# DeltaNet and a GELU layer on one core: chunk 5's squares at another place, chunk 1's tokens added on VectorE, chunk 1's joins two units at a time

## The chip, the core and the metric

The kernel runs on one core of a Trainium2 chip. The core has TensorE (matrix products, PE in the profile, its weight loads PEld), VectorE (DVE), ScalarE (ACT), GpSimd (POOL) and SyncE (SP, which issues most DMAs). Products are written to PSUM, and VectorE and ScalarE read them from there. The metric is the time of one execution on the device in microseconds.

## What is computed

A DeltaNet attention (4 batches, 8 heads, 768 steps, head size 48) is followed by two dense layers with an exact GELU between them:

```python
for t in range(S):
    kt, vt, bt = (k_n[:, :, t], v[:, :, t], beta[:, :, t, None])   # k_n = k / (|k| + 1e-6)
    y[:, :, t] = np.einsum('bhd,bhde->bhe', q[:, :, t], state)
    v_old = np.einsum('bhde,bhd->bhe', state, kt)
    state = state + bt[:, :, :, None] * np.einsum('bhd,bhe->bhde', kt, vt - v_old)
...
h = x @ w_in                       # x: y as 3072 tokens of 384; w_in 384 x 2048
g = 0.5 * h * (1.0 + erf(h * inv_sqrt2))
return (g @ w_out)                 # w_out 2048 x 384
```

Both weight matrices come as 64-bit floats and are decoded on the chip.

## The kernel before

The 768 steps are cut into 12 chunks of 64. A chunk has two units (`NA` = 2; unit `a` holds batches 2a and 2a+1 on the two halves of the partitions, with 8 heads). Two chunks form a pair `g`. For a pair, the products of keys with keys ("grams", `psG`) give triangular systems. Their 32x32 diagonal blocks are inverted on VectorE, row by row (`eliminate`, L489 to L503, then transposes L512 and L516). The off-diagonal 32x32 block is filled by two small levels of products, the "joins" (`psJ`): level 0 multiplies gram and inverse and is scaled by VectorE into `XM`; level 1 multiplies that with the inverse and is copied by ScalarE into `Zf`.

A chunk then goes through `against_state` (products of keys and queries with the state, `psK`; L661 to L668), `subtract` (L672: `W` = those of the keys minus V, on VectorE; `y` = those of the queries, copied by ScalarE), `solve` (`psU`), `use` (`psY`, and the state's update into the same tile), `next_state` (L748, VectorE) and `read` (L750: the tokens `x` out of `psY`). `turn` (L766) transposes x into `xT`, and the two dense layers follow. Chunk 0 has no state to read, so its `y` is empty. For chunk 1, x and y are kept apart and added on TensorE, by two products with the identity into one PSUM tile (L776). For later chunks, `read` adds y on VectorE and `turn` transposes once (L779).

The first joins of chunk 1 use `join` (L538): one product per unit, half and level, into a tile of the two-bank tag `dn`. The later pairs use `join_run` (L575): two neighbouring units in one product with 64 columns, of which the two diagonal blocks are read out, each by an instruction of its own; its level 1 copies are recorded with `put_off` and issued later by `copy_out`.

The norm of a chunk's keys, from chunk 4 on, takes three steps: `norms(c)` (L333: two ScalarE squares, one per unit, into `ksq` tiles that share the tag `x` with the tokens), `prep(c)` (L345: two row sums on VectorE, L349, and a power with exponent 0.5 on GpSimd, L351), and `finish(c)` for the pair (L303 to L307 on VectorE: reciprocals and the factors `gm`).

The two dense layers of chunks 0 and 1 are plain products (`fc1` L811, `fc2` L829). From chunk 2 on they are products of blocks with sums and differences of blocks (names P1 to R22 in `part_of_layer`, L906, products at L916; second layer at L859). The sums of the weights are VectorE's (L842, L846, L874). Product P4 writes on into the PSUM tile Y1, which VectorE's L947 must have read before; L939 and L968 read it earlier.

The order of the work is written by hand up to L1173. From L1196 on it is a plan: each step has a time on a scale in which chunk c's dense layers run from c+1 to c+2 (chunk 0's to 2.25), and all steps are issued in the order of these times. VectorE keeps that order as written; the other engines are ordered by a scheduler that follows it but may move an instruction that it takes to be ready ahead of one that isn't. ScalarE instructions issued through `keep` or `copy_out` stay in their order among themselves, and the products of `together` follow one another. Every engine runs its instructions in the final order. Weights of the first layer are decoded up to L1172 and from plan time 0.99 to 1.36, those of the second from 1.365 to 1.9 (VectorE L231 to L261, ScalarE L237).

Of the kernel before, what the change touches and what calls it, by code (L numbers as in the profile page):

```python
# [19 lines left out]
def kernel(  # L20
# [28 lines left out]
    nc = tc.nc  # L49
# [517 lines left out]
    def put_off(name, dst, src):  # L567
        copies[name].append((dst, src))
# [6 lines left out]
    def join_run(g, ts0, ts1):  # L575

        xm, zf, off = XMs[g], Zf[g % 2], Gs[g]
        gm = gms[g].rearrange("q t h -> q (t h)")
        sets = []
        both = dn("psJ") if g > 1 and ts0 else None  # L580
        for level, ts in enumerate((ts0, ts1)):
            if ts:
                if both is not None:
                    psJ = both[:, level]
                else:
                    psJ = small[0].tile([128, 512], F32, tag="sq" if level else "z", name="psJ")
                sets.append((level, ts[0] * H, psJ.rearrange("q (k n) -> q k n", n=2 * HB)))
        for k in range(H):
            for p in range(2):
                for level, u0, psJ in reversed(sets):  # L590
                    us = slice(u0 + 2 * k, u0 + 2 * k + 2)
                    rows = slice(p * C + level * HB, p * C + (level + 1) * HB)
                    nc.tensor.matmul(psJ[HALF[p], k, :],  # L593
                                     lhsT=(xm if level else off)[rows, us, :],
                                     rhs=zf[rows, us, HB:C] if level else xm[rows, us, :],
                                     start=True, stop=True)
        for level, u0, psJ in sets:
            for p in range(2):
                for e in range(2):
                    us = slice(u0 + e, u0 + 2 * H, 2)  # L600
                    at_ = p * C + e * HB
                    src = psJ[at_:at_ + HB, :, e * HB:(e + 1) * HB]
                    if level == 0:
                        low_ = slice(p * C + HB, (p + 1) * C)
                        nc.vector.tensor_tensor(
                            xm[low_, us, :], src,
                            gm[low_, us].unsqueeze(2).to_broadcast([HB, H, HB]), op=ALU.mult)
                    else:
                        put_off("join", zf[p * C:p * C + HB, us, HB:C], src)

    def gram_steps(c, part=(0,)):
        us = [tiles[c, a] for a in range(NA)]
# [38 lines left out]
    def against_state(us):  # L651

        for u in us:
            u.W = wk.tile([128, H, D], F32, tag="W", name="W")
            u.y = None
            if u.c == 0:
                nc.gpsimd.tensor_tensor(u.W, u.V,
                                        ng[:, u.a].unsqueeze(2).to_broadcast([128, H, D]),
                                        op=ALU.mult)
                continue  # L660
            u.psK = dn("psK")[:, :, 0:2 * NP * D].rearrange("q r (x j d) -> q x r j d", x=2, d=D)  # L661
            for x in range(2):
                for j in range(NP):
                    for r, p in QUADS:
                        rows = slice(r * C, r * C + D)
                        to = HALF[p ^ (j % 2)] if x and u.c > 1 else HALF[p]
                        nc.tensor.matmul(u.psK[to, x, r, j, :], lhsT=(u.Qt if x else u.Kt)[rows, p, j, :],  # L667
                                         rhs=St[rows, u.a, p ^ r, j, :], start=True, stop=True)  # L668
        if us[0].c > 2:
            subtract(us)  # L670
# [79 lines left out]
    def read(u, copy=nc.scalar.copy):  # L750
        u.x = wk.tile([128, H, D], F32, tag="x", name="x")
        both = slice(0, 128)
        for to, at_, s in ((both, both, 0), (HALF[0], HALF[1], 1), (HALF[1], HALF[0], 1)):
            dst, src = pairs(u.x[to], s), u.psY[s][at_]
            if u.c < 2:
                copy(dst, src)
            else:
                nc.vector.tensor_tensor(dst, src, pairs(u.y[at_], s), op=ALU.add)
# [7 lines left out]
    def turn(u):  # L766
        if u.a == 0:
            xTs[u.c] = wk.tile([128, NM, NA * 128], F32, tag="xT", name="xT")
        xT = xTs[u.c]
        psX = sq("psX", NM, 128)  # L770
        for m in range(NM):
            cols = slice(m * 128, (m + 1) * 128)
            if u.c == 1:

                for i, part in enumerate((u.x, u.y)):
                    nc.tensor.matmul(psX[:, m, :], lhsT=part.rearrange("q h d -> q (h d)")[:, cols],  # L776
                                     rhs=ident, start=i == 0, stop=i == 1)
            else:
                nc.tensor.transpose(psX[:, m, :], u.x.rearrange("q h d -> q (h d)")[:, cols], ident)  # L779
        nc.scalar.copy(xT[:, :, u.a * 128:(u.a + 1) * 128], psX)  # L780

    def turns(us):
# [271 lines left out]
    def at(first, last, steps):  # L1054

        total, done, timed = sum(s[0] for s in steps), 0.0, []
        for w, *step in steps:
            timed.append((first + (last - first) * (done + 0.5 * w) / total, step))
            done += w
        return timed  # L1060
# [128 lines left out]
    def state_at(c, *times, first=(), second=()):  # L1189

        steps = state_steps(c, first, second)
        if len(times) > len(steps):
# [4 lines left out]
    plan += [decode_in(), at(1.365, 1.9, decode_steps(n_in, NW)), at(1.91, 1.911, [(1.0, late)])]  # L1197
    rows1, join1 = eliminate_steps(1), join_steps(1)
    plan += [at(1.06, 1.065, [(1.0, load, 3)]),
             [(t, (join, 0, range(NA, 2 * NA), level)) for level, t in enumerate((1.085, 1.16))],  # L1200
]
    sums = [(1.0, sum_of_squares, tiles[3, a], h) for a in range(NA) for h in range(H)]
    plan += [at(1.48, 1.8, sums), at(1.81, 1.811, [(1.0, fn, c) for c in (2, 3) for fn in (norms, prep)]), at(1.9, 1.905, [(1.0, finish_both)]), at(2.725, 2.726, [(1.0, queries, third)]),
# [61 lines left out]
    for w in range(3, NC):  # L1265
        two_ahead = w + 2 < NC
        if w % 2:
            if w == 3:
                plan += [at(w + 0.19, w + 0.191, [(1.0, transposed, u, (1,)) for u in fourth]),
                         at(w + 0.1, w + 0.101, [(1.0, together, *gram(5))]),  # L1270
                         at(w + 0.06, w + 0.061, [(1.0, norms, 5), (1.0, prep, 5)]),
                         at(w + 0.11, w + 0.111, [(1.0, finish, 4)])]
                plan += rows_of(2, w, ((1, 0.112, 0.113), (2, 0.16, 0.2), (4, 0.224, 0.31),
                                       (2, 0.325, 0.365), (1, 0.395, 0.4), (2, 0.485, 0.5),
                                       (2, 0.508, 0.54), (5, 0.6, 0.685), (7, 0.76, 0.88),
                                       (3, 1.0, 1.05), (5, 1.07, 1.1), (1, 1.153, 1.154),
                                       (1, 1.2, 1.201), (1, 1.201, 1.202)))
            elif two_ahead:
                plan += rows_of(w // 2 + 1, w, ((1, -0.35, -0.349), (1, -0.34, -0.339),
                                                (1, -0.23, -0.229), (5, -0.22, -0.14),  # L1280
                                                (1, -0.07, -0.06), (3, 0.005, 0.05),
                                                (3, 0.068, 0.148), (2, 0.156, 0.215),
                                                (2, 0.235, 0.31), (3, 0.325, 0.365),
                                                (1, 0.398, 0.409), (2, 0.485, 0.5),
                                                (1, 0.508, 0.54), (5, 0.6, 0.685),
                                                (3, 0.76, 0.8), (1, 1.003, 1.004),
                                                (1, 1.16, 1.161), (1, 1.166, 1.167)))
            plan += [state_at(w, w + 0.367, w + 0.59, w + 0.72, w + 0.93, second=query(w))]
        else:
            j0, j1, j2 = join_steps(w // 2)  # L1290
            t = w + (0.25 if w == 4 else 0.165)
            plan += [at(t, t + 0.001, [(1.0, together, j0, *query(w))]),
                     at(w + 0.37, w + 0.371, [(1.0, together, j1, *gram(w + 2))]),
                     state_at(w, w + 0.465, w + 0.58, w + 0.72, w + 0.93, second=[j2] + gram(w + 3))]
            plan += spread("join", 4, w + 0.395)
            plan += spread("join", 4, w + 0.64)
            if two_ahead:
                plan += spread("gram", 2, w + 0.375) + spread("gram", 2, w + 0.42)
                plan += spread("gram", 4, w + 0.63)
                plan += [at(w + 0.366, w + 0.367, [(1.0, norms, w + 2)]), at(w + 0.3715, w + 0.372, [(1.0, prep, w + 2)]),  # L1300
                         at(w + 0.56, w + 0.561, [(1.0, norms, w + 3), (1.0, prep, w + 3)]),
                         at(w + 0.64, w + 0.641, [(1.0, finish, w + 2)])]
# [32 lines left out]
```

## Time and profile before

| | |
|---|---|
| time, median of 3 runs | 646.0 us (645.03 to 646.12) |
| the profiled execution | 644.96 us, of which the span is 643.2 us |
| TensorE busy (matmul) | 617.9 us, 96% of the span, 9702 records |
| VectorE busy | 496.3 us, 77%, 1011 instructions |
| ScalarE busy | 259.9 us, 40%, 586 instructions |
| GpSimd busy | 66.0 us, 10%, 58 instructions |
| mean granted TensorE clock | 0.985 |

The page gives the busy share in 40 equal slices of 16.1 us, in tenths:

```profile
PE   6759999999989999999999999999999999999997
DVE  6999989989589997999577999577999565354342
ACT  4576767524632256132266132266132253132230
POOL 4044002001301003001003001013001000000000
PEclk9987999999989999999999999999999999999999
```

The first 160 us hold the hand-written start, the decoding of the weights and chunks 0 and 1; then chunks 2 to 11 follow with TensorE nearly always busy. A matmul of 32-bit floats shows as two records in the trace, a transpose as one.

### The profile page before, as it was taken

What the parts mean: (1) busy time and instruction counts of PE and PEld (TensorE: products, weight loads), DVE (VectorE), ACT (ScalarE), POOL (GpSimd) and SP (SyncE); (2) the same over time, 40 slices, a digit from 0 to 9 for tenths busy, and PEclk for the clock granted to TensorE, in tenths of its full rate; (3) what the DMA queues carried; (4) which work ended last, traced back from release to release, by engine and by line L of the source; (5) the groups of instructions that cost most, each with busy time, mean ns of one, the idle gap of its engine ahead of it and who ended that gap; (6) DMA issues with size and microseconds to landing.
All of it is one profiled execution on the core that took longest, in us unless ns stands there. A gap on an engine that the chain in (4) does not pass through costs nothing.

```text
span 643.2 us, 22156 instructions
## 1 busy us (share of the span) xinstructions
PE 617.9 (96%) x9702; PEld 573.8 (89%) x9702; DVE 496.3 (77%) x1011; ACT 259.9 (40%) x586; POOL 66.0 (10%) x58
## 2 busy tenths in 40 slices
PE   6759999999989999999999999999999999999997
PEld 5658876776879999999999999999999999999997
DVE  6999989989589997999577999577999565354342
ACT  4576767524632256132266132266132253132230
POOL 4044002001301003001003001013001000000000
PEclk9987999999989999999999999999999999999999
DMA  9794683204422335312325312411211400100100
GB/s 135 174 273 159 129 199 113 45 1 74 84 37 42 56 43 91 58 24 37 66 34 86 61 21 41 67 21 33 51 25 35 69 3 3 25 2 3 25 2 24
DMA packets 158433, 39.79 MB, mean 62 GB/s; under 512 B 150016, under 2 KB 153216, under 8 KB 158336
## 3 DMA queue, kind: packets, MB, share of 16 engines
q1 hardware_dynamic: 155664, 37.34, 30.0%
q10 hardware_dynamic: 2672, 1.03, 0.8%
q8 instruction: 76, 1.25, 0.8%
q14 instruction: 21, 0.17, 0.1%
HBM read 33.62 MB, written 4.72 MB: 60 GB/s over the span
## 4 chain that ended last, share of the span: by engine, by line
PE 77%; DVE 14%; DMA 2%; issue 2%; SPq 2%; ACT 1%; POOL 1%; DVEq 0%; POOLq 0%
PE psX L859 12%; PE psY L916 11%; PE psY L859 8%; PE psX L916 8%; PE psV L916 5%; PE psZ L916 5%; PE psZ L859 4%; PE psV L859 4%; PE psK L667 3%; DVE Nu L503 3%; DVE tmp L501 3%; PE psG L414 3%; PE psJ L593 3%; PE psH L811 2%; PE psY L732 2%
## 5 line engine op out<-in xcount | busy, mean ns | idle before, releaser
L916 PE MATMUL psX<-xT,w_in_sb 128*128 128x128 f32 x480 | 64.8, 278 | 0.0
L503 DVE TENSOR_TENSOR Nu<-Nu,tmp 128x58 f32<-128x58 f32 (+13 forms) x168 | 57.9, 344 | 5.8
L501 DVE TENSOR_TENSOR tmp<-Nu 128x58 f32<-128x58 f32 (+13 forms) x168 | 58.0, 345 | 4.4
L916 PEld LDWEIGHTS psX<-xT,w_in_sb 128*128 128x128 f32 x480 | 59.4, 193 | 0.9
L902 ACT COPY xT<-psX 128x768 f32<-128x768 f32 x9 | 7.2, 799 | 124.3 <-PE psX L788 124.3
L351 POOL TENSOR_TENSOR n<-n,half 128x16 f32<-128x16 f32 x10 | 31.4, 3145 | 251.8 <-DVE n L349 191.2
L859 PE MATMUL psX<-w_out_sb,G 128*128 128x192 f32 x320 | 55.3, 326 | 0.0
L859 PEld LDWEIGHTS psX<-w_out_sb,G 128*128 128x128 f32 x320 | 52.1, 190 | 0.0
L811 PE MATMUL psH<-xT,w_in_sb 128*128 128x256 f32 x192 | 45.2, 390 | 0.5 <-ACT G L902 0.4
L829 PE MATMUL psO<-w_out_sb,G 128*128 128x384 f32 x128 | 43.9, 490 | 0.0
L811 PEld LDWEIGHTS psH<-xT,w_in_sb 128*128 128x128 f32 x192 | 36.3, 193 | 8.0 <-ACT G L902 1.3
L916 PE MATMUL psY<-xT,w_in_sb 128*128 128x128 f32 x320 | 43.1, 279 | 0.0
L916 PEld LDWEIGHTS psY<-xT,w_in_sb 128*128 128x128 f32 x320 | 39.8, 196 | 0.0
L902 ACT COPY pu<-psZ 128x512 f32<-128x512 f32 x40 | 23.5, 587 | 39.3 <-PE psZ L916 37.7
L829 PEld LDWEIGHTS psO<-w_out_sb,G 128*128 128x128 f32 x128 | 23.6, 190 | 14.0
L902 ACT ACTIVATE G<-G 128x512 f32<-128x512 f32 x40 | 25.2, 630 | 23.3 <-DVE G L947 22.6
L939 DVE TENSOR_TENSOR psY<-psY,pu 128x512 f32<-128x512 f32 x20 | 14.0, 698 | 22.4 <-PE psY L916 19.6
L376 POOL TENSOR_TENSOR V<-V,n 128x384 f32<-128x384 f32 x18 | 17.0, 959 | 135.4 <-DMA V<-in_v_dram 115.5
L859 PE MATMUL psZ<-T,pu 128*128 128x192 f32 x160 | 28.6, 332 | 0.0
L859 PE MATMUL psY<-T,G 128*128 128x192 f32 x160 | 28.6, 332 | 0.0
L859 PE MATMUL psV<-w_out_sb,G 128*128 128x192 f32 x160 | 27.7, 326 | 0.0
L859 PE MATMUL psX<-T,G 128*128 128x192 f32 x160 | 27.6, 326 | 0.0
(183 smaller groups left out, 1346.1 us busy)
## 6 DMA issues: line engine op xcount, KB each, us to landing
Kp<-in_k_dram SPq DMA_DIRECT2D x76, 96.0 KB, 3.2
w_out_sb<-in_moe_w_in_dram SPq DMA_DIRECT2D x24, 256.0 KB, 4.1
w_raw<-in_moe_w_out_dram SPq DMA_DIRECT2D x16, 384.0 KB, 4.5
V<-in_v_dram SPq DMA_DIRECT2D x48, 96.0 KB, 3.1
out_dram<-o_sb SPq DMA_DIRECT2D x40, 96.0 KB, 2.2
Qp<-in_q_dram SPq DMA_DIRECT2D x64, 32.0 KB, 2.1
Qp<-in_q_dram SPq DMA_DIRECT2D x16, 96.0 KB, 4.7
Qp<-in_k_dram SPq DMA_DIRECT2D x32, 32.0 KB, 2.2
```

The lines of the kernel that those rows point to most:

```text
L351: nc.gpsimd.tensor_tensor(flat, flat, half, op=ALU.pow)
L376: engine.tensor_tensor(u.V, u.V, ns[u.c][:, u.a].unsqueeze(2).to_broadcast([128, H, D]), op=ALU.mult)
L414: nc.tensor.matmul(psG[HALF[p], r, i * NP + j, :], lhsT=u.Kt[rows, p, j, :], rhs=(u.Qt if x else u.Kt)[rows, p, j, :], start=True, stop=True)
L501: nc.vector.tensor_tensor(tmp, nu[:, j + 1:, j:j + 1].to_broadcast([128, n, j]), nu[:, j:j + 1, 0:j].to_broadcast([128, n, j]), op=ALU.mult)
L503: nc.vector.tensor_tensor(nu[:, j + 1:, 0:j], nu[:, j + 1:, 0:j], tmp, op=ALU.add)
L593: nc.tensor.matmul(psJ[HALF[p], k, :], lhsT=(xm if level else off)[rows, us, :], rhs=zf[rows, us, HB:C] if level else xm[rows, us, :], sta ...
L667: nc.tensor.matmul(u.psK[to, x, r, j, :], lhsT=(u.Qt if x else u.Kt)[rows, p, j, :], rhs=St[rows, u.a, p ^ r, j, :], start=True, stop=True)
L811: nc.tensor.matmul(psH, lhsT=w_in_sb[:, f // 2, m, f % 2 * 128:(f % 2 + 1) * 128], rhs=xTs[c][:, m, :], start=(m == 0), stop=(m == NM - 1))
L829: nc.tensor.matmul(u.psO, lhsT=G[:, u.a, f, :], rhs=w_out_sb[:, f, :], start=(f == 0), stop=(f == NF - 1))
L859: nc.tensor.matmul(ps_, lhsT=lhs[:, f, :], rhs=rhs[:, f, :], start=first and f == 0, stop=f == FH - 1, skip_group_check=not first)
L902: i = fn(*args, **kw)
L916: nc.tensor.matmul(ps_[:, i], lhsT=lhs[:, f // 2, f % 2 * 128:(f % 2 + 1) * 128], rhs=rhs, start=first and i == 0, stop=True, skip_group_c ...
```

## The change

The squares and row sums of chunk 5 are put at other plan times: `norms(5)` from 3.06 to 2.93, right behind chunk 2's turn (2.922), and `prep(5)` from 3.06 to 2.961, right behind `last_sum_of_w` (L846, 2.96). `finish(4)` stays at 3.11, `sum_of_w(4)` (L842) at 3.07.

Chunk 1's tokens are read like those of later chunks: `read` adds y on VectorE (six additions in place of six ScalarE copies), `turn` transposes x alone, and `against_state` puts the query products of chunk 1 on the partitions that this addition needs.

Chunk 1's two joins (plan times 1.085 and 1.16, unchanged) use `join_run`, with PSUM tiles of the one-bank tag `sq`, and their level 1 copies are issued at once.

```diff
@@ join_run
-                    psJ = small[0].tile([128, 512], F32, tag="sq" if level else "z", name="psJ")
+                    psJ = small[0].tile([128, 512], F32, tag="sq" if level or g == 0 else "z",
+                                        name="psJ")
...
-                        put_off("join", zf[p * C:p * C + HB, us, HB:C], src)
+                        put = put_off if g else lambda name, to, at: nc.scalar.copy(to, at)
+                        put("join", zf[p * C:p * C + HB, us, HB:C], src)
@@ against_state
-                        to = HALF[p ^ (j % 2)] if x and u.c > 1 else HALF[p]
+                        to = HALF[p ^ (j % 2)] if x and u.c > 0 else HALF[p]
@@ read
-            if u.c < 2:
+            if u.c < 1:
                 copy(dst, src)
             else:
                 nc.vector.tensor_tensor(dst, src, pairs(u.y[at_], s), op=ALU.add)
@@ turn
-            if u.c == 1:
-
-                for i, part in enumerate((u.x, u.y)):
-                    nc.tensor.matmul(psX[:, m, :], lhsT=part.rearrange("q h d -> q (h d)")[:, cols],
-                                     rhs=ident, start=i == 0, stop=i == 1)
-            else:
-                nc.tensor.transpose(psX[:, m, :], u.x.rearrange("q h d -> q (h d)")[:, cols], ident)
+            nc.tensor.transpose(psX[:, m, :], u.x.rearrange("q h d -> q (h d)")[:, cols], ident)
@@ the plan
-             [(t, (join, 0, range(NA, 2 * NA), level)) for level, t in enumerate((1.085, 1.16))],
+             [(1.085, (join_run, 0, range(NA, 2 * NA), ())),
+              (1.16, (join_run, 0, (), range(NA, 2 * NA)))],
...
-                         at(w + 0.06, w + 0.061, [(1.0, norms, 5), (1.0, prep, 5)]),
+                         at(w - 0.07, w - 0.069, [(1.0, norms, 5)]), at(w - 0.039, w - 0.038, [(1.0, prep, 5)]),
```

In the last lines w is 3.

## The prediction

> **What bounds the kernel now.** I read the busy times by stretch first, then TensorE's waits, then each engine's timeline around the three places of the change. The stretches (columns: stretch, length, busy time and instruction count of TensorE matmul, TensorE load, VectorE, ScalarE, GpSimd, granted TensorE clock, DMA share, GB/s):
>
> ```profile
> 71.50:88.00 16.50, 16.47 (x369) 14.11 (x370) 14.70 (x23) 13.03 (x28) 0.00 (x0) 1.00 0.62 116
> 93.00:110.00 17.00, 17.00 (x62) 11.32 (x62) 16.70 (x24) 11.41 (x36) 2.94 (x1) 1.00 0.52 160
> 176.00:180.00 4.00, 0.01 (x1) 0.00 (x0) 3.83 (x8) 0.01 (x1) 1.61 (x2) 1.00 0.38 46
> 180.00:184.50 4.50, 4.49 (x25) 4.49 (x26) 4.36 (x7) 1.69 (x3) 0.00 (x0) 0.62 0.35 42
> 184.50:260.00 75.50, 75.50 (x1453) 73.17 (x1453) 66.11 (x139) 31.36 (x64) 9.79 (x6) 1.00 0.35 54
> ```
>
> TensorE is full nearly everywhere. It stands still once, from 176 to 180, and pays again afterwards: its clock is granted at 0.62 in the next 4.5 us. From 93 to 138 VectorE is as full as TensorE. The hole at 176, on GpSimd, VectorE and TensorE (start, us, engine, line, operation, wait before it):
>
> ```profile
> 168.60 0.70 DVE L939 TENSOR_TENSOR psY<-psY,pu 128x512 f32<-128x512 f32 x1 [2.77 <-ACT diag L425]
> 169.40 0.69 DVE L968 TENSOR_TENSOR pu<-psY,pu 128x512 f32<-128x512 f32 x1
> 170.40 1.01 DVE L349 TENSOR_REDUCE n<-ksq 128x8 f32<-128x384 f32 x2 [0.30 <-ACT ksq L902]
> 171.33 1.75 DVE L842 TENSOR_TENSOR T<-w_out_sb,T 128x1536 f32<-128x1536 f32 x1
> 175.87 0.18 DVE L303 TENSOR_SCALAR n<-n 128x32 f32<-128x32 f32 x1 [2.79 <-POOL n L351]
> 179.27 0.68 DVE L947 TENSOR_TENSOR G<-psY,pu 128x512 f32<-128x512 f32 x1
> ...
> 171.49 4.35 POOL L351 TENSOR_TENSOR n<-n,half 128x16 f32<-128x16 f32 x1 [10.76 <-DMA Kp<-in_k_dram]
> ...
> 180.01 1.56 PE L916 MATMUL psY<-TX,w_in_sb 128*128 128x128 f32 x8 [4.00 <-DVE G L947]
> ```
>
> This is chunk 5's norm: squares on ScalarE at 169.84, row sums on VectorE (L349), the square root as a power on GpSimd (L351), then VectorE's factors (L303). L947, which frees the PSUM tile that product P4 needs, is queued behind the factors on VectorE, so TensorE waits 4.00 us. The power's releaser is named as a DMA, but the row sums end at 171.41, 0.08 us before it: they are the real releaser. VectorE also idled 2.77 us at 168.60.
>
> Chunk 1's tokens (ScalarE reads them out, TensorE turns x and y) and the next join:
>
> ```profile
> 86.79 0.56 DVE L748 TENSOR_TENSOR St<-St,psY 128x384 f32<-128x384 f32 x1 [1.21 <-PE psY L743]
> 87.72 0.56 DVE L748 TENSOR_TENSOR St<-St,psY 128x384 f32<-128x384 f32 x1 [0.38 <-PE psY L743]
> 88.20 0.95 DVE L260 SCALAR_TENSOR_TENSOR w_e<-w_raw,w_e 128x768 uint32<-128x768 uint32 x1
> ...
> 137.95 1.15 PE L593 MATMUL psJ<-XM,G 32*64 32x64 f32 x32 [0.48 <-DVE XM L512]
> ```
>
> From 88.20 VectorE decodes weights and then eliminates, without a gap over 0.25 us, until TensorE waits 0.48 us for it at 137.95.
>
> [...] Here the three transposes of chunk 2's unit take 0.33 us (160.98 to the next product at 161.31), the twelve matmul records of chunk 1's unit 1.34 us (88.98 to 90.32). [...] the power took 4.35 us beside L842, which reads two SBUF tensors, and 2.90 us at 157.82, with nothing of the kind beside most of it.
>
> **Part A, the squares sooner.** It moves two ScalarE squares (0.94 us) from behind chunk 4's grams to behind chunk 2's turn, the two row sums (1.01 us) and the power from behind L968 to behind L846; no DMA is issued with them. Chunk 5's keys are there: their four loads are issued from 149.59 to 153.52 and land 2.8 to 4.0 us later. The squares' buffers are chunk 2's x tiles, free after the transposes (last start 162.04). So the squares run from about 163.1, in a ScalarE gap of 1.46 us before 164.56. Row sums: L846 ends at 165.83, so 165.85 to 166.87, inside VectorE's 2.77 us idle time before 168.60; hidden, and if that cover were gone it would cost 1.0. Power: 166.9 to 169.8 at 2.90 (171.3 at 4.35). L842 then follows L968 at 170.1 and ends at 171.85; both powers are done by then, so the factors start at 171.87 instead of 175.87: 4.0 us. From there to L947's end is 179.95-175.87 = 4.08 us, so P4 may start at 176.0. TensorE's previous product (174.95, 1.06 long) ends at 176.0 too. The 4.0 us wait goes. The cold tail goes too: from 180.01 to 184.42 three groups of eight took 4.41 us, where a warm group goes every 0.89 (185.31 to 186.21): 4.41-2.67 = 1.7 us. What is late next: VectorE gains only 4.0 where TensorE gains 5.7, and at 228.77 the next join needs VectorE's transpose, which ends at 228.36. VectorE has 0.93 (L939 at 186.48) and 0.38 (190.25) of idle time to catch up; 0.4 slack and 1.3 idle cover 1.7. I charge 0.2. The earlier squares also release the key buffers for SP's next loads (171.00) earlier, which nothing waits for. Part A: -5.5, between -5.7 and -4.0 (tail kept).
>
> **Part B, tokens and Y added on VectorE.** Off ScalarE: six copies, 1.96 us, beside its other work, worth nothing. On VectorE: six adds, for which chunk 2's L758 is the row: 1.08 and 1.09, together 2.17. They stand in the queue between the two state additions and ahead of L260; 0.38 of it falls into the wait before 87.72. So VectorE's decode is late by 1.8. Off TensorE: 2 x (1.34-0.33) = 2.0. New waits: x waits for VectorE instead of ScalarE (second unit ready at 90.0, formerly 89.3), and w_out's second decoded block, used at 90.32, is ready at 91.9 instead of 90.1. TensorE may stand there up to 2.6 us unless other products are ordered ahead of it. That TensorE runs full from 93 to 137.5 makes its saved 2.0 worth something only if the join at 137.95 isn't governed by VectorE. It is: VectorE comes at 137.8+1.8 = 139.6. Behind the join VectorE had one wait on TensorE, 1.15 us at 145.06, which can take up part. Cost: from +0.4 (that wait absorbs 1.15 and part of the filler is ordered ahead) to +1.9, and below nothing (-0.5) only if the products' order lets the saved 2.0 through. I take +1.1. The other PSUM half for Y (L666) costs nothing: same products.
>
> **Part C, joins with two units to a product.** TensorE: 64 records in 1.13 us (60.83 to 61.96) become 32 in about 1.07 (137.95 to 139.02), twice: -0.1. VectorE: two multiplications of 0.70 become four of 0.42-0.43: +0.33, in front of the second join, for which TensorE waits already (0.48 at 66.12). ScalarE: two copies of 0.58 become four of 0.36: +0.3, mostly in the 0.33 idle before 68.85. VectorE's extra is swallowed by its 1.21 us wait at 86.79. The psJ tile moves to a tag idle from 55 to 88. Cost 0 to +0.4; I take +0.2.
>
> **Sum.** -5.5+1.1+0.2 = -4.2 on the profiled execution (644.96 us, span 643.2), so 640.8. The shown median is 646.0, 1.0 above it; I forecast against the median: 641.8.
>
> **Rivals.** (1) Part A yields less because the chain is only moved: the power slow, or L842 and the factors still later than P4, a second hole of some 2 us. For it: VectorE is 99% full around there. Against it: 2.77 us idle ahead of it. A is then about -3.3, net -2.0: 644.0. (2) Both parts gain: TensorE's saved 2.0 is used, because the products are ordered anew around the join, so B is -0.5 and A -5.7; net -6.2, 639.8. Against it: VectorE is just as full. (3) Slower: the start-up becomes VectorE's, with new holes in TensorE at 66, 89 and 136, each followed by a cold tail of 1.7 as at 180. Price: 1.8+0.3+3 x 1.7 = 7.2, against -5.5: +1.7, 647.7. It decides once each hole passes the idle time that the clock tolerates (between 1 us, which left it at 1.00 at 66, and 4.0). Against it: holes at 89 and 136 are 2.6 and some 4 us at most if nothing fills them, and products of the dense layers are there to fill them.
>
> **How the numbers follow.** Forecast 0.66, rival 1 0.16, rival 2 0.08, rival 3 0.10. About 0.2% (1.3 us) is what this kernel's measurement tells from no change. Of rival 1, 0.06 lies within it, of rival 3 0.02: faster 0.84, same 0.08, slower 0.08. The forecast's own ends are 646.0-5.3 = 640.7 and 646.0-1.7 = 644.3; the range reaches a little to rival 2: 640.0 to 644.6.
>
> **What would show it.** Right: chunk 5's squares near 163, power before 170, P4 with no wait over 0.3 us and a granted clock near 1.00 after 176; six L758 adds at 87 to 90 on VectorE; the join of 137.95 some 0.5 to 2 us later. Wrong: a wait on L947 or L303 that stays, a new TensorE hole over 3 us at 89 or 136 with a lowered clock behind it, or the join at 228 waiting over 0.5 us for VectorE.

## The result, and the profile after

The changed kernel takes 645.68 us in the median, the kernel before 645.7 us, each in 19 runs taken side by side. The ratio is 0.9991 with a 95% interval of 0.9982 to 0.9999: a gain of some 0.6 us, of 1.2 us at most by the interval, where 4.2 us were forecast. The profiled execution has the same span as before, 643.2 us. The runs of the changed kernel spread over 3.35 us (643.58 to 646.93), those of the kernel before over 1.64 us.

The hole at 176 is gone. The busy times of the changed kernel by stretch (columns as in the prediction: TensorE matmul and load, VectorE, ScalarE, GpSimd, granted clock, DMA share, GB/s):

```profile
138.00:164.40 26.40, 24.40 (x547) 17.59 (x548) 21.71 (x29) 9.06 (x21) 1.29 (x1) 0.87 0.23 43
...
176.00:180.00 4.00, 4.00 (x38) 4.00 (x37) 3.83 (x7) 3.21 (x6) 1.61 (x2) 1.00 0.58 108
180.00:184.50 4.50, 4.50 (x42) 4.50 (x41) 4.46 (x5) 2.56 (x5) 0.00 (x0) 1.00 0.31 39
```

From 176 to 184.5 TensorE is full and its clock is whole, where it stood and then ran at 0.62. But the stretch from 138 to 164.4 now has 2.0 us of idle TensorE and a clock of 0.87. The timeline of the changed kernel shows both places (start, us, engine, line, operation, and the wait before it):

```profile
89.22 1.09 DVE L760 TENSOR_TENSOR x<-psY,y 128x192 f32<-128x192 f32 x3
90.34 0.96 DVE L260 SCALAR_TENSOR_TENSOR w_e<-w_raw,w_e 128x768 uint32<-128x768 uint32 x1
137.88 1.97 DVE L512 STREAM_TRANSPOSE XM<-Nu 128x1024 f32<-128x1024 f32 x1
140.00 1.15 PE L594 MATMUL psJ<-XM,G 32*64 32x64 f32 x32 [2.95 <-DVE XM L512]
141.08 0.72 PE L669 MATMUL psK<-St,Kt 48*64 48x48 f32 x32
142.43 1.08 PE L669 MATMUL psK<-St,Kt 48*64 48x48 f32 x32
144.29 4.88 PE L825 MATMUL psO<-w_out_sb,G 128*128 128x384 f32 x8
...
168.28 0.94 ACT L898 ACTIVATE ksq<-Kp 128x384 f32<-128x384 f32 x2
169.64 1.05 PE L912 MATMUL psX<-xT,w_in_sb 128*128 128x128 f32 x8
171.03 1.01 DVE L349 TENSOR_REDUCE n<-ksq 128x8 f32<-128x384 f32 x2
172.11 2.90 POOL L351 TENSOR_TENSOR n<-n,half 128x16 f32<-128x16 f32 x1 [6.10 <-DVE n L349]
176.95 0.17 DVE L303 TENSOR_SCALAR n<-n 128x32 f32<-128x32 f32 x1
181.13 1.12 PE L912 MATMUL psY<-TX,w_in_sb 128*128 128x128 f32 x8
183.87 1.06 PE L912 MATMUL psZ<-TX,Sw 128*128 128x128 f32 x8
```

The same places in the kernel before:

```profile
135.71 2.09 DVE L512 STREAM_TRANSPOSE XM<-Nu 128x1024 f32<-128x1024 f32 x1
139.52 0.65 PE L667 MATMUL psK<-St,Qt 48*64 48x48 f32 x32
141.03 2.85 PE L829 MATMUL psO<-w_out_sb,G 128*128 128x384 f32 x8
164.36 1.05 PE L916 MATMUL psX<-xT,w_in_sb 128*128 128x128 f32 x8
184.42 1.06 PE L916 MATMUL psZ<-TX,Sw 128*128 128x128 f32 x8
```

Read the lower half of the changed kernel's lines first. The squares start right behind chunk 2's turn, the power takes 2.90 us and ends at 175.01, the factors (L303) follow L838 with no wait, and P4 follows the product ahead of it with no wait. From the first product P1 of chunk 2 to P5 of the second block it is 14.23 us (169.64 to 183.87), before 20.06 (164.36 to 184.42): the squares gain 5.83 us.

Now the upper half. VectorE takes up its decode at 90.34 instead of 88.20. It reaches the transpose L512 at 137.88 instead of 135.71. The join that waits for it starts at 140.00 instead of 137.95, and TensorE stands for 2.95 us instead of 0.48. Behind the join TensorE is slow: each 32 records of psK take 0.85 us from start to start (142.43 to 143.28) instead of about 0.47, and the eight records of psO 4.88 us instead of 2.85.

P1 of chunk 2 starts 5.28 us later than before. That splits as follows. The join is 2.05 us late; 0.37 of that is there already at VectorE's first addition to chunk 1's state (87.16 instead of 86.79), ahead of the tokens, and 1.7 come behind it. From the join's start to the start of the next join it takes 9.09 us (140.00 to 149.09) instead of 5.86 (137.95 to 143.81), 3.23 us more. From there to P1 it is 20.55 us in both. So 5.28 us are lost before P1 and 5.83 gained behind it. The 0.55 us that remain at P5 are lost again by the end (459.3 us from P5 to the end of the span, before 458.8).

### The profile page after: what moved, and what is told of

It reads as the page before. It is cut to its first block, busy times and chain, and to the rows that moved or that the text cites. A ratio compares the mean times of both kernels' runs of the same rounds, so it can differ in the third digit from the quotient of the medians.

```text
span 643.2 us, 21991 instructions
## 1 busy us (share of the span) xinstructions
PE 620.4 (96%) x9620; PEld 573.9 (89%) x9620; DVE 498.3 (77%) x1019; ACT 257.8 (40%) x582; POOL 64.7 (10%) x58
## 4 chain that ended last, share of the span: by engine, by line
PE 78%; DVE 16%; issue 2%; ACT 1%; DMA 1%; POOL 0%; SPq 0%; DVEq 0%; ACTq 0%; POOLq 0%
PE psX L855 12%; PE psY L912 11%; PE psX L912 8%; PE psY L855 8%; PE psV L912 5%; PE psZ L912 5%; PE psZ L855 4%; DVE tmp L501 4%; DVE Nu L503 4%; PE psV L855 4%; PE psK L669 4%; PE psO L825 3%; PE psG L414 3%; PE psJ L594 3%; PE psU L704 2%
## 5 line engine op out<-in xcount | busy, mean ns | idle before, releaser
L825 PE MATMUL psO<-w_out_sb,G 128*128 128x384 f32 x128 | 46.5, 510 | 0.3 <-DVE w_out_sb L261 0.2
L807 PE MATMUL psH<-xT,w_in_sb 128*128 128x256 f32 x192 | 46.5, 395 | 0.2
```

Of the source, the lines that this page charges most:

```text
L807: nc.tensor.matmul(psH, lhsT=w_in_sb[:, f // 2, m, f % 2 * 128:(f % 2 + 1) * 128], rhs=xTs[c][:, m, :], start=(m == 0), stop=(m == NM - 1))
L825: nc.tensor.matmul(u.psO, lhsT=G[:, u.a, f, :], rhs=w_out_sb[:, f, :], start=(f == 0), stop=(f == NF - 1))
```

## The experiments

Theory 1: the squares gain in full. The tokens on VectorE make the join near 138 late, TensorE stands ahead of it for so long (2.95 us) that its clock falls behind the hole, and the slow products there cost more than the lateness itself. Theory 2: there is no such step. Either only VectorE's lateness counts, or the hole at 176 was never worth its 5.8 us.

All kernels were profiled and timed beside the kernel before. Profiled executions of one source differ by up to 1.5 us already at the end of the hand-written start (the join of the squares alone starts at 138.13 in one and 139.65 in the other), so the table gives lengths within one execution. "Wait" is TensorE's idle time right ahead of the join near 138. "Join to P1" is the time from that join's start to P1 of chunk 2. "P1 to P5" reaches to P5 of the second block.

| kernel | ratio to before (95%) | wait | join to P1 | P1 to P5 |
|---|---|---|---|---|
| before | 1 | 0.48 | 26.41 | 20.06 |
| changed | 0.9991 (0.9982 to 0.9999) | 2.95 | 29.64 | 14.23 |
| squares alone | 0.9902 (0.9889 to 0.9915) | 0.49 | 26.42 | 14.22 |
| tokens alone | 1.0060 (1.0048 to 1.0072) | 2.94 | 29.63 | 20.05 |
| joins alone | 1.0012 (1.0004 to 1.0020) | 0.49 | 27.08 | 20.93 |
| tokens and joins | 1.0100 (1.0084 to 1.0115) | 2.98 | 29.56 | 20.05 |
| squares and joins | 0.9925 (0.9911 to 0.9940) | 0.49 | 27.47 | 14.23 |
| changed, hole filled idly | 0.9932 (0.9920 to 0.9944) | 0.44 | 26.46 | 14.22 |
| changed, join after 8 records more | 0.9931 (0.9912 to 0.9950) | 0.45 | 24.89 | 14.23 |
| squares, VectorE delayed | 0.9948 (0.9931 to 0.9964) | 1.15 | 26.42 | 14.23 |
| changed, one product in the hole | 0.9982 (0.9969 to 0.9994) | 2.29 | 29.67 | 14.22 |
| changed, two products in the hole | 0.9988 (0.9976 to 1.0001) | 1.69 | 29.60 | 14.23 |
| squares and tokens, join later | 0.9907 (0.9892 to 0.9923) | 0.45 | 24.89 | 14.23 |
| squares alone, again | 0.9908 (0.9893 to 0.9923) | 0.50 | 26.41 | 14.23 |

### The parts one by one

The squares alone is the kernel before with this edit:

```diff
-                         at(w + 0.06, w + 0.061, [(1.0, norms, 5), (1.0, prep, 5)]),
+                         at(w - 0.07, w - 0.069, [(1.0, norms, 5)]), at(w - 0.039, w - 0.038, [(1.0, prep, 5)]),
```

> The kernel before with the squares of chunk 5 moved and nothing else. Theory 1 (the start-up of chunks 0 and 1 gave back what the squares gained: the join near 138 waits for VectorE and the TensorE clock falls behind that wait): the whole gain stays, 5.0 to 5.7 us, ratio 0.991 to 0.9925; the join at 138 waits about 0.5 us as before and the granted clock from 138 to 164 is 1.00. Theory 2 (the hole at 176 was never worth time, its gain is lost later to VectorE): ratio 0.999 to 1.000.

The tokens alone has the edits of `against_state`, `read` and `turn`:

> The kernel before with chunk 1's tokens added on VectorE and turned once, nothing else. Theory 1: the join near 138 waits 2 to 3 us, the products behind it run slow, and P1 of chunk 2 comes 4 to 5.5 us late; ratio 1.006 to 1.0085, and the 4 us wait at 176 is still there, moved. Theory 2 (only VectorE's own delay counts, the clock has no part): P1 late by 1.5 to 2.2 us, ratio 1.0025 to 1.0035.

The joins alone has the edits of `join_run` and of the two plan lines 1.085 and 1.16:

> The kernel before with chunk 1's joins two units to a product, nothing else. Theory 1: within 0.4 us of before, ratio 0.9994 to 1.0008. Rival (the joins lengthen the hole at 138 enough to let the clock fall): ratio 1.004 or more.

The changed kernel with `norms(5)` and `prep(5)` back at 3.06:

> The changed kernel with the squares left at their place. Theory 1: the loss of the start-up in full plus the old wait at 176: 4.5 to 6 us slower than before, ratio 1.007 to 1.0095. Theory 2 (the parts don't add up; the squares moved cause the early loss): ratio 0.999 to 1.002.

Measured: 640.13 us in the median against 646.63 for the squares alone, a gain of 6.3 us by the ratio, slightly beyond what was expected; P1 to P5 shrinks by the full 5.84 us and the join's stretch is that of before. The tokens alone lose 3.9 us by the ratio, tokens and joins together 6.5, which is more than the 4.5 to 6 expected. In both the wait is near 2.95 us and join to P1 is 3.2 us longer, and the old wait at P4 (4.0 us) is still there. The profile of the tokens alone shows the slow products although the squares are at their old place:

```profile
139.46 1.15 PE L593 MATMUL psJ<-XM,G 32*64 32x64 f32 x32 [2.94 <-DVE XM L512]
142.86 1.09 PE L667 MATMUL psK<-St,Qt 48*64 48x48 f32 x32
143.88 4.74 PE L823 MATMUL psO<-w_out_sb,G 128*128 128x384 f32 x8
```

So most of the loss belongs to the tokens, and the squares' gain stands by itself. Theory 2's second form is out. The joins alone were expected within 0.4 us and cost 0.8 (ratio 1.0012), without a longer wait ahead of the join. Their P1 to P5 is 20.93 us, 0.87 longer than before, in the one execution that was profiled: there the slow clock behind P4's wait lasted longer (see "How long a hole"). The squares with the joins:

> The changed kernel with chunk 1's tokens left on ScalarE and turned twice. Theory 1: like the squares alone, 5 to 5.7 us faster than before, ratio 0.991 to 0.993. Rival (the joins matter): 1 us or more slower than that.

By the ratio they are 1.5 us slower than the squares alone (1.1 us slower than these in their second trial), with intervals that overlap. That is what the rival named, though not clear of noise; join to P1 is 1.05 us longer. Of the joins alone and of these two together the profile shows one more pause, inside psK, with nothing awaited; here that of squares and joins:

```profile
140.57 0.52 PE L669 MATMUL psK<-St,Qt 48*64 48x48 f32 x23
141.90 0.37 PE L669 MATMUL psK<-St,Qt 48*64 48x48 f32 x9 [0.81 <-issue]
```

It is 0.42 us in the joins alone, in the same place (after 23 of 32 records). The kernels that have the tokens on VectorE as well don't show it. Its cause was not found. Yet there, too, the joins cost time: tokens and joins are 2.6 us slower by the ratio than the tokens alone, clear of both intervals, while the profiled executions of the two differ by 0.3 us (that of tokens and joins was the fastest of its six runs). Where that loss lies stays open.

### The hole filled with products that nothing reads

```diff
+    def warm():
+        psW = small[0].tile([128, DM], F32, tag="sq", name="psW")
+        for f in range(4):
+            nc.tensor.matmul(psW, lhsT=G[:, 0, f, :], rhs=w_out_sb[:, f, :], start=f == 0, stop=f == 3)
...
-             at(2.595, 2.596, [(1.0, together, join1[0])]),
+             at(2.595, 2.596, [(1.0, together, (warm,), join1[0])]),
```

> The changed kernel with four more products (eight records, about 2.6 us) into a PSUM tile that nothing reads, put on TensorE right ahead of the join near 140. Theory 1 (the clock): the join starts no later than in the changed kernel, near 140.0, the products behind it run at full clock, P1 of chunk 2 comes 2.5 to 3.2 us earlier; ratio to before 0.994 to 0.9955. Theory 2 (VectorE's lateness alone is the price): nothing gained, ratio 0.998 to 1.000.

```profile
136.89 2.74 PE L1199 MATMUL psW<-w_out_sb,G 128*128 128x384 f32 x8
140.08 1.15 PE L594 MATMUL psJ<-XM,G 32*64 32x64 f32 x32 [0.44 <-DVE XM L512]
141.15 0.68 PE L669 MATMUL psK<-St,Kt 48*64 48x48 f32 x32
143.17 2.89 PE L825 MATMUL psO<-w_out_sb,G 128*128 128x384 f32 x8
```

The join starts at 140.08, as late as in the changed kernel. Yet psK and psO run at their old pace, join to P1 is 26.46 us, and the kernel takes 642.26 us, 0.68% less than before and a little less than Theory 1 had expected. P1 starts at 166.54 instead of 169.64. TensorE did more work and the kernel became faster: this is the test that separates the clock from the lateness. Its runs lie within 0.68 us (641.70 to 642.38), where those of the changed kernel spread over 3.35.

### The hole filled with work that has to be done

```diff
-             at(2.595, 2.596, [(1.0, together, join1[0])]),
+             at(2.656, 2.6565, [(1.0, together, join1[0])]),
-             at(2.65, 2.651, [(1.0, sum_of_w_in, 1)]), ...
-             at(2.6, 2.601, [(1.0, together, (against_state, third))]),
+             at(2.6605, 2.661, [(1.0, sum_of_w_in, 1)]), ...
+             at(2.657, 2.6575, [(1.0, together, (against_state, third))]),
```

> The changed kernel with the join near 140 and the products against the state behind it put after the next eight records of the second layer (2.65 us of TensorE work that formerly followed them), and one weight sum of VectorE behind the join's scaling as before. Theory 1 (the hole and its cold clock are the loss): the hole is filled with work that has to be done, so the saved 2 us of TensorE and the clock both come back; P1 of chunk 2 starts 3.5 to 5 us earlier than in the changed kernel, ratio to before 0.991 to 0.9935. Theory 2 (VectorE is the bound): ratio 0.997 to 1.000.

The ratio is 0.9931 and join to P1 is 24.89 us. The 2.65 us of products that were moved no longer lie behind the join, but join to P1 is shorter by only 1.5 us than the 26.4 of before: TensorE now waits behind the join, the longest time 0.68 us for ScalarE's copy of `y`. The same edit without the joins:

> The squares moved and chunk 1's tokens on VectorE, the hole before the join near 138 filled with eight records of the second layer that have to be done anyway, and chunk 1's joins left as before. If VectorE bounds the start-up once the hole is filled, it equals the squares alone within 0.5 us (P1 near 164.5); if the saved 2 us of TensorE come through, it is 1 to 2 us faster than that.

> The kernel before with the squares moved, again, beside the one above on the same chip: ratio 0.990 to 0.992.

Both take the same: 640.43 and 640.01 us. With the hole filled, the tokens on VectorE are neither a loss nor a gain. TensorE's saved 2 us bought nothing: P1 starts 77.8 and 77.9 us behind VectorE's first addition to chunk 1's state, and TensorE stands for 1.7 us in between instead of 0.6. That VectorE sets the pace there fits, but no run made VectorE faster. With the joins as well, the kernel is 1.5 us slower again (0.9931 against 0.9907, the intervals overlap). The squares alone is the simplest kernel that beats the kernel before and the changed one, by 0.8 to 1.0%.

### VectorE late, TensorE not sooner

Six additions whose result nothing reads, on VectorE, in the kernel with the squares moved:

```diff
             next_state(u)
             read(u)
+            if u.c == 1:
+                for rows in (slice(0, 128), HALF[0], HALF[1]):
+                    t = wk.tile([128, HB * HB // 4], F32, tag="tmp", name="tmp", bufs=1)
+                    part = u.y[rows].rearrange("q h d -> q (h d)")[:, 0:192]
+                    nc.vector.tensor_tensor(t[rows, 0:192], part, part, op=ALU.add)
```

> The kernel before with the squares moved, and six additions on VectorE whose result nothing reads put where the change adds its six (chunk 1's tokens stay on ScalarE and are turned twice). It has VectorE's delay of about 2 us, but not TensorE's saved 2 us. Theory 1a (the saved TensorE time itself lengthens the hole and tips the clock): the join waits 2 us or less, the clock stays at or near 1.00, ratio 0.9935 to 0.996. Theory 1b (VectorE's delay is enough to tip it): the join waits 2 to 3 us, the clock falls, ratio 0.998 to 1.000.

In the profiled execution the wait is 1.15 us and the clock holds (1.00 from 137 to 165, join to P1 26.42). VectorE is as late as in the changed kernel: the join starts 52.9 us behind VectorE's first addition to chunk 1's state in one, 52.8 us in the other, and 51.4 to 51.5 us with the squares alone. But TensorE ends the products ahead of the join 1.8 us later than in the changed kernel (51.7 us behind that addition instead of 49.9), and that is the difference between the holes of 1.15 and 2.95 us. So in these executions the delay alone costs its own length, and it takes the saved TensorE time on top to make the hole in which the clock fell. The saving was not only worth nothing there, it did harm.

The timed runs are less clear. By the ratio the kernel is 3.0 us slower than the squares alone (0.9948 against 0.9902), twice the 1.5 us by which the join is late. Three of its six runs, among them the profiled one, take 641.64 to 641.75 us, the other three 643.46 to 643.70. None of the slower three was profiled. A slow clock in them is possible and not shown; so it isn't shown either that a hole of 1.15 us always leaves the clock whole.

### How long a hole

The filling with one and with two products in place of four:

> The changed kernel with one more product (two records, 0.65 us) ahead of the join near 140, so that TensorE stands there about 2.3 us instead of 2.95. The clock theory leaves open where the limit lies between 1.15 us (no fall seen) and 2.94 us (falls in all four kernels that had it): if 2.3 us is still too long, ratio 0.998 to 1.000 and P1 of chunk 2 near 169; if not, 0.993 to 0.995 and P1 near 166.5. The rival without a clock says no difference from the changed kernel.

> As the last, with two more products (1.3 us), a stand of about 1.65 us. Clock theory: more likely no fall, ratio 0.993 to 0.995, P1 near 166.5; if the limit is below 1.65 us, 0.998 to 1.000. Without a clock: no difference from the changed kernel.

In both the clock still falls, and in the second it was expected not to. (A hole of 2.94 us or more had brought the fall in three kernels, not in four.) With a hole of 1.69 us join to P1 is 29.60 us, nearly the same as with 2.95. The stretches between the changes of the clock, first of the kernel with two products, then of the kernel before and of the joins alone behind P4's wait of 4.00 us, last of the changed kernel with the join later (columns as above):

```profile
138.41:141.82 3.41, 1.72 (x38) 1.07 (x36) 3.38 (x4) 0.00 (x0) 0.00 (x0) 1.00 0.00 0
141.82:148.65 6.83, 6.83 (x135) 5.32 (x134) 4.64 (x7) 2.09 (x2) 0.00 (x0) 0.50 0.02 5
...
180.61:184.02 3.41, 3.41 (x18) 3.41 (x18) 3.34 (x5) 1.08 (x3) 0.00 (x0) 0.50 0.38 45
...
180.68:187.50 6.82, 5.80 (x27) 5.80 (x28) 6.33 (x12) 1.92 (x4) 0.00 (x0) 0.50 0.31 37
...
139.55:142.96 3.41, 3.28 (x161) 3.12 (x161) 3.32 (x5) 1.55 (x2) 0.00 (x0) 1.00 0.02 5
142.96:146.38 3.42, 3.31 (x70) 2.39 (x70) 3.33 (x5) 1.99 (x5) 0.00 (x0) 1.00 0.02 5
```

The clock is whole in the hole itself and half behind it. (The 0.87 and 0.62 further up are averages over whole and half.) In all five kernels with a fall at the join it is half for 6.83 us. At half clock eight records of psY take 1.71 us (joins alone, 183.57 to 185.28), at whole clock 0.90 (the same product in the changed kernel, 182.08 to 182.98). Work that gets half a clock for 6.83 us loses some 3.4 us, an estimate, half of 6.83; join to P1 is longer by 3.15 to 3.26. Behind P4's wait the half clock lasts 3.41 us in three of the four profiles that have this wait (before, tokens alone, tokens and joins), which fits the 1.7 us of the prediction, and 6.83 us in the fourth, the joins alone, with the same wait of 4.00 us.

These lengths are steps. In the changed kernel the clock rises at 59.67, falls at 141.59 and rises at 148.42: 81.92 and 6.83 us, which is 24 and 2 times 3.41. From one change to the next it is 4, 36, 1 and 134 times 3.41 us in the kernel before, 5, 24, 2 and 145 times in the changed one. In the five other profiles in which the clock falls again behind the start-up, that fall lies 25 times (joins alone: 36 times) 3.41 us behind the rise ahead of it, to within 0.2 us. Where these windows of 3.41 us lie, counted from the start of the kernel, differs from execution to execution: the rise is at 59.67 in the changed kernel and at 57.73 in the kernel before. Behind the joins alone's wait the first window at half clock begins at 180.68 and P4 only at 181.70, so 1.02 us of this window were still empty, and the clock stayed half for another. In the kernel before P4 starts at 180.01, ahead of the fall at 180.61; the window behind the fall is full, and the clock is whole after it. So the same hole of 4.00 us cost one window in three executions and two in the fourth: its length alone doesn't set the price. That its place in the windows does is a reading of these few executions.

What a window held before the clock fell can be read off, too. At the join, TensorE stood for 1.48 to 2.41 us in the window just ahead of the fall and worked mostly on the small products of the joins and psK, with at most 0.61 us of large ones. In nine profiles a window near 62, in which TensorE also stood for 1.51 to 1.60 us but worked on large products (psH) for most of the rest, left the clock whole (1.00 from 60 to 71.5). And the last two lines above show a window with 3.28 us of small products and none large, with hardly a gap: the clock stayed whole. So neither 1.6 us of standing nor the small products alone were enough here; standing of that length and small products in one window were, in each of the five profiles.

The timed runs of the two kernels with one and two products spread from 642.4 to 648.6 us. That would fit a fall that comes in some executions and not in others, as the windows lie, but only one execution of each was profiled, so this isn't shown. Nor is it shown that a limit for the length of a hole lies between 1.15 and 1.69 us.

## Why the prediction was wrong

**Part A was right.** The squares ran in ScalarE's gap, the power took 2.90 us where it had taken 4.35, the factors and L947 came in time for P4. Named: 4.0 for the wait, 1.7 for the tail, less 0.2 for VectorE near the later join. Measured: 5.83 from P1 to P5 in the changed kernel, and 6.3 by the ratio for the squares alone. Rival 1 is out.

**Part B failed in its price.** The sum took +1.1. VectorE's own delay was sized well: the decode was to be late by 1.8; from the first addition to the state on, the join came 1.7 late. Two steps of the price went wrong. First, the term for the cold clock was missing from it. The prediction named a hole at 136 of "some 4 us at most" and a restart of 1.7, but put them only into rival 3, and set the limit, an estimate from two places of the trace, between 1 us and 4.0 (from 60 to 71.5 TensorE stands for 0.97 us in all, the longest waits are 0.48 and 0.39). The clock fell at 2.95, and the restart costs 3.2 at this place, nearly twice the 1.7 of the one at 180, because the half clock lasted two windows of 3.41 us instead of one. TensorE's saved 2.0 us were counted as worth nothing at the join, not as what lengthens the hole. Second, the forecast let the wait of 1.15 us at 145.06 and a new order of the products take up part of the delay. Neither happened: TensorE's order around the join stayed as it was, with psO's eight records behind it, and VectorE's wait for the next join grew to 4.40 us because the products between the joins were slow. Measured, the tokens alone cost 3.9 us by the ratio, where at most 1.9 were named.

**Part C** was taken at +0.2. On VectorE it adds the 0.33 us that were named (1.74 for the scaling instead of 1.41). But in the four pairs of kernels that differ in the joins alone it costs 0.8, 1.5, 2.6 and 1.5 us by the ratio, of which two are clear of noise (0.8 and 2.6). So this term was too small as well. A pause that the profile doesn't explain is a part of it in two of these kernels; the rest stays open.

**A reading.** The prediction set 0.33 us for three transposes beside 1.34 us for twelve records. These twelve records are six products, two for each block, as x and y were turned apart. For one block turned once it is 0.11 us against 0.22, a factor of two. The saving of 2.0 us doesn't hang on this.

**The rivals.** Rival 3 had the mechanism, a hole made by VectorE and a cold tail (products at the lowered clock) behind it, at one of its three places. There it cost more than its 1.7, and elsewhere nothing: the hole at 89 was filled, because the scheduler put other products there (TensorE stands for 0.17 us from 88 to 93), and the one at 66 stayed as short as it was (0.51 us instead of 0.48). With 5.28 us lost at one place and 5.83 gained at another the two parts cancelled, which no case of the forecast had. Rival 2 could not be: the saved 2.0 us of TensorE don't count while VectorE is last to arrive, and the one other order that was tried, with the join put later, didn't change it.

## What to carry to other kernels

Where two engines reach a meeting point at nearly the same time, work taken from the one that would arrive first was not a saving here. It lengthened TensorE's wait (2.95 us, where VectorE's delay alone made 1.15), and the slow clock behind that wait cost another 3.23 us. So price a hole on TensorE as its length plus a possible slow stretch behind it, here one or two windows of 3.41 us at half clock, that is 1.7 or some 3.2 us. Holes of 1.69 to 2.98 us with small products around them had one in each of the five profiles; the length of the hole alone doesn't tell. Look for work that can be put into it: four products that nothing read brought P1 forward by 3.1 us here. And try the parts of a change one by one: two large effects of opposite sign look like a change that does nothing.

## What the runs showed of the hardware

In the kernel before and the changed one the granted TensorE clock was whole (1.00) or half (0.50), and from one change to the next it is a whole multiple of 3.41 us (1 to 145 times). No window ahead of a fall at the join or at P4 was idle throughout. At the join the clock fell behind windows in which TensorE stood for 1.48 to 2.41 us and ran small products (32 to 48 rows) for most of the rest, around waits of 2.94 to 2.98 (three kernels), 2.29 and 1.69 us; at P4's wait it fell behind windows with 2.81 to 3.24 us of standing. It did not fall around the wait of 1.15 us in the one execution profiled, nor in windows with 1.51 to 1.60 us of standing and large products otherwise, nor in one with 3.28 us of small products alone. While the clock was half, a window with 3.41 us of small products (141.82 to 145.24 in the kernel with two products) was followed by another at half. Each of these falls lasted one or two whole windows and cost 1.7 us (the wait of 4.00 us at 176; 0.87 us more in the joins alone) or 3.15 to 3.26 us (the five kernels with a fall at the join).
